# Starting the next group's frequency stage inside the end of the sort, and leaving out the filler matmuls ahead of the first expert tile

## The chip, the cores and the metric

The kernel runs on one core of a Trainium2 chip. The metric is the device time of one execution in microseconds (us); three runs of the kernel before have a median of 2162.24 us (2158.75 to 2167.45). The core has five engines that run their own instruction queues in order: PE (matrix products, with PEld for its weight loads), DVE (vector work), ACT (copies, activations), POOL (elementwise work and the indirect scatters) and SP (issues nearly all plain DMAs). They meet only through semaphores.

## The reference, cut to what matters

```python
# x: (8, 5696, 128)  h: (5696, 128)      L = 2 * 5696
Xf = np.fft.rfft(x, n=L, axis=1); Hf = np.fft.rfft(h, n=L, axis=0)
y = np.fft.irfft(Xf * Hf[None], n=L, axis=1)[:, :S]        # causal convolution
tok = y.reshape(8 * 5696, 128)
e = argmax(tok @ w_gate)                                   # one expert of 8 per token
p = softmax(tok @ w_gate)[e]
out[token] = p * (relu(tok @ w1[e]) @ w2[e])               # w1 128x1024, w2 1024x128
```

## The kernel before, in words

The eight batches are cut into three groups of 2, 3 and 3 (g = 0, 1, 2). The convolution of a group runs in three stages. `phase_a` (for g = 1 and 2 as a `Guest`) multiplies by the 119-point matrix and stores U to DRAM. `phase_b` is the 48-point stage: 120 frequencies, for g = 1 and 2 one per step; four frequencies share one set of loads (`load_m`: the matrix `mt`; `load`: the data `uq` of 576 KB, the inverse matrix `mi` twice 72 KB, the filter `hh` twice 192 KB). A step n issues the forward matmul of frequency n (`forward`, tile `xp`), the DVE product of frequency n - 1 (three operations, the first writes `zt`), the sum of n - 2, the inverse matmul of n - 4 (`vp`) and the copy of n - 5, and then yields to the planner. `phase_c` is the second 119-point stage, which here is called the sort: it makes the tokens, computes logits, ranks every token within its expert, and scatters the rows with POOL into the sorted array SR.

The expert layers (`pipeline`) work on tiles of 256 sorted rows, four steps to a tile (k = 0 to 3). A step does six `mh` matmuls (first layer), the ACT and DVE halves of the relu (`hs`), and six `ma` matmuls (second layer) of two steps earlier. The four quarters of an expert's weights are loaded by `load_w` (`wb`, 512 KB each); from the second tile on, each of these loads is conditional and moves nothing when the tile has the same expert as the one before. `load_w` reads two registers from a table on SP first. There is one set of weight buffers in the parts concerned here, so a load can be issued only when the tile before has passed the quarter that it overwrites.

The order of the instructions on every engine is fixed when the program is built. `run` (L1346) holds the streams `rest` (phases B and C), the weight preparation and `experts`, each with a clock of its own; it always advances the one whose clock is lowest and adds to its clock the cost that it yields (an expert step costs STEP = 1420). What a stream issues before the next yield is one block in program order. Inside `phase_c` a sub-step issues its matmuls, yields, and then does the copies and the ranking of that sub-step. The sort of g = 0 has sub-steps at = 0 to 31 with fresh data and ends with 32, 33, 34, 36 and 38; that of g = 1 has 0 to 47 and ends with 48, 49, 50, 52 and 54. `finished` is the sub-step at which the guest (phase A of the next group) was done: 31 for g = 0, 46 for g = 1. Beginning the next group's `phase_b` (`after`) takes place at L943: two calls of `next(after)`, each of which issues one set of loads. In g = 0 these are in sub-steps 36 and 38, in g = 1 in 50 and 52. Its steps begin after the sort, in the loop at L974.

`spin` (L227) issues matmuls on constants into a PSUM bank that nobody reads: 22 at the start of the first `phase_b`, 40 ahead of the transposition of the first expert tile (L1308), 24 ahead of its first layer (L1301).

Names used below for the expert tiles at the end of the second sort, in order: V, W, X, Y. X has the expert of W; Y has another one, so its weights are really loaded.

Of the kernel before, what the change touches and what calls it, by code (L numbers as in the profile page):

```python
# [59 lines left out]
HOLD = 3  # L60
FETCHED = (0, 1)
GUESTED = (0,)
EAGER = (2, 0)
SETTLED = (2840, 8000, 8000)
LEAD = (0, 4, 6)
A3 = (True, True, True)
# [4 lines left out]
LOGIT = (2, 2, 2)  # L71
RARE = 3
XR = 7
SPIN = (22, 40, 24)


@with_exitstack
def conv_moe(ctx: ExitStack, tc: tile.TileContext, I, out, B, S, D, E, F, split):
# [148 lines left out]
    def spin(count):  # L227
        bank = ps.tile([P, 512], F32, tag="cx", name=f"spin{spun[0]}", bufs=4)
        spun[0] += 1
        for k in range(count):  # L230
            nc.tensor.matmul(
                bank, fcr[:, 0, 0], fcr.rearrange("p a c q -> p (a c q)"), start=True, stop=True
            )
# [220 lines left out]
    def phase_b(gr, guest=None):  # L454
        g, cb, cw, nch, QB, QW = gr.g, gr.cb, gr.cw, gr.nch, gr.qb, gr.qw
# [136 lines left out]
            if g:  # L592
                yield STEP * HEAD[g] / 2
        if g == 0:
            spin(SPIN[0])
        for qb in range(2 if g == 0 else 0):
            for k in range(QB):
                filt(qb, k)
# [92 lines left out]
    def phase_c(gr, guest=None, after=None):  # L691
        g, nb, cb, cw, NI, ns = gr.g, gr.nb, gr.scb, gr.scw, gr.ni, gr.ns
# [9 lines left out]
        nu = NB // NI  # L702

        def load(n):
            if n >= nu:
                return
            vq = sb.tile([PR, 2, NI, gr.cols], F32, tag="ld", name=f"vq{g}_{n}", bufs=LD)
            if g:
                nc.sync.dma_start(vq.rearrange("q c i x -> q (c i) x"), gr.V[:, 2 * n * NI : 2 * (n + 1) * NI, :])
            else:  # L710
                nc.sync.dma_start(vq, gr.V.rearrange("q (c i) x -> q c i x", c=2)[:, :, n * NI : (n + 1) * NI, :])
            vqs[n] = vq.rearrange("q c i x -> q c (i x)")
# [186 lines left out]
        finished, ahead = [None], [0]  # L899
# [4 lines left out]
        for n in range(n_end + 1):  # L904
            for k in range(nsub):
                at = n * nsub + k
                if parts[0].ready and state["prepped"]:
                    state["alone"] = False
                if k == 0:
                    load(n + 2)  # L910
                made = turning = read = carried = None
                if n < nu:
                    made = synth(n, k)
                if TL <= at < total_sub + LL:
                    tp = bank(f"tp{g}_{n}_{k}", "mh")
                if 0 <= at - TL < total_sub:
                    turning = turn(*divmod(at - TL, nsub), tp)
                whole = 0 <= at - LL < total_sub and (at - LL) % nsub == nsub - 1
                if whole:
                    for j in range(nsub):  # L920
                        spare = tp if j else ybank.get((n, k))
                        if spare is None:
                            spare = bank(f"lp{g}_{n}_{k}", "mh")
                        read = logit((at - LL) // nsub, j, spare)
                if k == 0 and n >= sl:
                    score(n - sl, n - sl - 1)
                if guest:
                    few = n < QUIET[g] or k == 0 and n >= sl and not state["alone"] and g
                    carried = guest.begin(1 if few else 2)
                ties = [made, read, carried] if carried and read else [made, turning, read or carried]  # L930
                ties = [x for x in ties if x is not None]
                count = 3 if len(sorts) > 8 else PER_SUB[g]
                for x in ties if len(ties) <= count else ties[:1] + ties[len(ties) - count + 1 :]:
                    sort_one(x)
                if state["alone"]:
                    yield cost if n < nu else cost / 2
                else:
                    yield STEP * (BESIDE if n < nu else ENDING)[g]
                if guest:
                    guest.end()  # L940
                    if guest.m >= guest.M and not guest.over and guest.done():
                        finished[0] = at
                if finished[0] is not None and at >= finished[0] + 4 and n >= nu - EAGER[g] and ahead[0] < 2:  # L943
                    next(after)
                    ahead[0] += 1
                if n < nu:
                    divide(*divmod(at + AHEAD, nsub))
                    settle(n, k)
                if 0 <= at - TL < total_sub:
                    turned(*divmod(at - TL, nsub))  # L950
                for j in range(nsub if whole else 0):
                    logit_out((at - LL) // nsub, j)
                if k == 0:
                    chains = []
                    if 0 <= n - sl - 1 < nu:
                        chains.append(rank(n - sl - 1))
                    if 0 <= n - sl < nu:
                        chains.append(route(n - sl))
                    zipped(*chains)
                    if n - sl - 1 in closes:  # L960
                        pt = closes[n - sl - 1]
                        chores.append(tables(pt, state["base"]))
                        if pt is parts[-1]:
                            chores.append(fill(pt, state["base"]))
                chore(3 if state["alone"] is False else 10)
                if at >= total_sub + LL:
                    break
# [296 lines left out]
    def pipeline(lo, hi):  # L1264
        LAG = 2
        step, nrow, nw, turned = (lo, 0), lo, (lo, 0), lo
        seen, hist, passed = {}, [None] * (LAG + 1), {}
        while True:
            t, k = step
            while nw[0] < min(t + 3, hi) and known(nw[0]):  # L1270
                was, n = user[nw[0]], nw[1]
                if home(nw[0]) and not state["spare"]:
                    break
                if was is not None and was >= lo and passed.get((was, n // 2), -1) < 2 * (n % 2) + 1:
                    break
                load_w(nw[0], n)
                nw = (nw[0], n + 1) if n < 3 else (nw[0] + 1, 0)
            while nrow < min(t + 4, hi) and usable(nrow):
                load(nrow)
                seen[nrow] = len(hist)  # L1280
                nrow += 1
            act = step if t in xts and nw > (t, k // 2) else None
            hist.append(act)
            old, done = hist[-1 - LAG], hist[-2 - LAG]
            to = done[0] if done and done[1] == NPAIR - 1 else None
            ti = turned if turned < nrow and seen[turned] + 2 <= len(hist) else None
            if ti is not None and (act and k < LAG or ti > t + 1 or act is None and ti > t):
                ti = None
            if act is None and old is None and to is None and ti is None:
                state["acting"] = False  # L1290
                leave(len(hist))
                recall(len(hist))
                deliver()
                if t >= hi and not (any(hist[-1 - LAG :]) or pending or leaving or staged or coming or returned):
                    return
                busy = pending or leaving or staged or coming or returned or turned < nrow or any(hist[-1 - LAG :])
                yield STEP if busy else None
                continue
            leave(len(hist))
            recall(len(hist))  # L1300
            if act and step == (0, 0):  # L1301
                spin(SPIN[2])
            if act:
                layer1(t, k)
                state["acting"] = True
                passed[t, 0] = k
            if ti == 0:
                spin(SPIN[1])  # L1308
            if to is not None or ti is not None:
                turn(to, ti)  # L1310
            if old:
                layer2(*old)
                passed[old[0], 1] = old[1]
            yield STEP
            done = None
            if act:
                done = relu(t, k)
                step = (t, k + 1) if k < NPAIR - 1 else (t + 1, 0)
                if k == NPAIR - 1:
                    xts.pop(t)  # L1320
            if ti is not None:
                turned_in(ti)
                turned += 1
            if old and old[1] == NPAIR - 1:
                drain(old[0])
            if to is not None:
                emit(to, len(hist))
            deliver(done)
# [140 lines left out]
```

## Time and profile before

| | before |
|---|---|
| median of three runs | 2162.24 us |
| profiled execution: its time / its span | 2152.79 us / 2151.1 us |
| busy PE, DVE, POOL, ACT | 95%, 72%, 59%, 51% |
| granted TensorE clock, mean | 0.992 |
| PE idle in the span | 2151.1 - 2051.9 = 99 us |

Busy shares are of the span. A row of the timeline gives the start, the time until the last of the merged instructions ended, the engine (SPq is SP's DMA issue), the line, the operation and its tiles, the count, and in brackets how long the engine stood idle ahead of it and for what. A granted clock of 1.00 is 2.4 GHz and 0.5 is 1.2 GHz; a value between is a mean of stretches at the two.

### The profile page before, as it was taken

The page shows a single profiled execution, that of the slowest core. Times are in us where ns is not written, and L with a number is a line of the kernel's source. Part 1 is how long each engine was busy: PE and PEld are TensorE (multiplying, and loading weights), DVE is VectorE, ACT ScalarE, POOL GpSimd, SP SyncE. Part 2 cuts the span into 40 slices and gives each one's busy share as a digit, 9 for nine tenths or more (in the row PEclk, how much of TensorE's full clock was granted, in tenths as well). Part 3 has the DMA queues.
Part 4 walks back from the last instruction along what each step waited for, and adds up shares of the span by engine and source line. Part 5 has one row for each costly group of instructions (what it writes and reads, how often), then busy time and mean ns, then how long its engine had stood idle before and what let it go on. Part 6 is the DMA issues. An engine that isn't in the chain of part 4 may idle for free.

```text
span 2151.1 us, 47076 instructions
## 1 busy us (share of the span) xinstructions
PE 2051.9 (95%) x14284; PEld 1758.3 (82%) x14284; DVE 1557.7 (72%) x3731; ACT 1104.0 (51%) x2359; POOL 1262.3 (59%) x1399
## 2 busy tenths in 40 slices
PE   8899888899999999989999999999999999999998
PEld 5788655666667888876777779999989999999998
DVE  4598745599998789879988885777775555555554
ACT  5688644333334666643434445666644454545444
POOL 6366446466665288882565662688876444444443
PEclk9999999999999999999999999999999999999999
DMA  9899998699998788777898986667645543444441
GB/s 349 280 318 319 316 390 309 197 268 277 285 283 252 281 285 275 260 224 214 243 260 247 253 254 225 209 212 215 199 147 178 170 140 112 140 141 144 144 143 35
DMA packets 236901, 494.39 MB, mean 230 GB/s; under 512 B 33553, under 2 KB 146446, under 8 KB 236647
## 3 DMA queue, kind: packets, MB, share of 16 engines
q1 hardware_dynamic: 212279, 443.06, 65.8%
q0 software_dynamic: 24368, 48.29, 7.0%
q8 instruction: 116, 1.90, 0.4%
q14 instruction: 138, 1.13, 0.2%
HBM read 598.31 MB, written 176.80 MB: 360 GB/s over the span
## 4 chain that ended last, share of the span: by engine, by line
PE 30%; issue 14%; POOL 10%; DVE 7%; DMA 6%; ACT 1%; SPq 1%; POOLq 0%; DVEq 0%; ACTq 0%
PE mh L1164 9%; PE ma L1185 8%; POOL out L1240 8%; PE yp L742 3%; PE vp L564 3%; DMA wb<-WD 3%; PE xp L528 3%; DMA SR<-rt,pi 2%; PE pa L315 2%; POOL SR L656 1%; PE mx L183 1%; DVE hs L1172 1%; PE tp L183 1%; POOL c_fcs L650 1%; ACT hs L1170 1%
## 5 line engine op out<-in xcount | busy, mean ns | idle before, releaser
L1172 DVE SCALAR_TENSOR_TENSOR hs<-mh,hs 128x512 fp32r<-128x512 f32 x728 | 501.1, 690 | 368.9 <-ACT hs L1170 363.9
L1164 PE MATMUL mh<-xtb,wb 128*128 128x256 f32 x4368 | 684.9, 292 | 24.9 <-DMA wb<-WD 12.6
L1170 ACT ACTIVATE hs<-mh 128x512 fp32r<-128x512 f32 x728 | 435.6, 599 | 449.0 <-PE mh L1164 438.0
L1164 PEld LDWEIGHTS mh<-xtb,wb 128*128 128x128 f32 x4368 | 581.6, 189 | 92.2 <-issue 29.4
L1185 PE MATMUL ma<-hs,wb 128*128 128x256 f32 x4368 | 651.5, 285 | 4.5 <-DMA wb<-WD 4.4
L1185 PEld LDWEIGHTS ma<-hs,wb 128*128 128x128 f32 x4368 | 564.4, 189 | 6.3 <-DMA wb<-WD 6.2
L656 POOL DMA_INDIRECT SR<-rt,pi x384 | 398.6, 1038 | 207.3 <-issue 61.9
L1240 POOL DMA_INDIRECT out<-xr x250 | 244.4, 977 | 313.1 <-DVE xr L1203 265.2
L555 POOL TENSOR_TENSOR zt<-zt,xs 128x384 f32<-128x384 f32 (+1 forms) x280 | 298.7, 1076 | 116.2 <-DVE xs L547 87.1
L579 ACT COPY vt<-vp 96x384 f32<-96x384 f32 (+1 forms) x300 | 149.1, 497 | 339.2 <-PE vp L564 332.4
L564 PE MATMUL vp<-zt,mi 128*96 128x384 f32 (+1 forms) x720 | 257.5, 453 | 8.0 <-DVE xs L547 5.6
L528 PE MATMUL xp<-uq,mt 96*128 96x384 f32 (+1 forms) x720 | 256.9, 452 | 3.7 <-ACT vt L579 1.7
L540 DVE TENSOR_TENSOR zt<-xp,hh 128x384 f32<-128x384 f32 (+1 forms) x300 | 173.9, 580 | 47.6 <-PE xp L528 32.5
L564 PEld LDWEIGHTS vp<-zt,mi 128*96 128x96 f32 x720 | 112.4, 162 | 100.6 <-issue 51.0
L1240 POOL DMA_INDIRECT out<-xb x114 | 111.3, 976 | 133.1 <-ACT hs L1170 107.4
L547 DVE SCALAR_TENSOR_TENSOR xs<-xp,hh 64x384 f32<-64x384 f32 (+1 forms) x300 | 175.9, 586 | 6.1
L545 DVE TENSOR_TENSOR xs<-xp,hh 64x384 f32<-64x384 f32 (+1 forms) x300 | 173.3, 578 | 6.0
L315 PE MATMUL pa<-xc,fcr 120*128 120x512 f32 x576 | 166.5, 420 | 10.1 <-DVE rk L867 2.8
L528 PEld LDWEIGHTS xp<-uq,mt 96*128 96x128 f32 x720 | 120.8, 190 | 33.3 <-issue 13.4
L315 PEld LDWEIGHTS pa<-xc,fcr 120*128 120x128 f32 x576 | 101.4, 192 | 43.5 <-DVE rk L867 8.0
L650 POOL TENSOR_TENSOR c_fcs<-c_fcs 120x64 f32<-120x64 f32 (+1 forms) x288 | 126.4, 439 | 6.8
L330 DVE COPY ut<-pa 128x512 f32<-128x512 f32 x96 | 65.8, 687 | 84.5 <-PE pa L315 80.7
(137 smaller groups left out, 2330.1 us busy)
## 6 DMA issues: line engine op xcount, KB each, us to landing
wb<-WD SPq DMA_DIRECT2D x728, 512.0 KB
vq<-VU SPq DMA_DIRECT2D x64, 768.0 KB
VU<-ut SPq DMA_DIRECT2D x48, 768.0 KB
uq<-VU SPq DMA_DIRECT2D x60, 576.0 KB
VU<-vt SPq DMA_DIRECT2D x60, 576.0 KB
xt<-x SPq DMA_DIRECT2D x96, 256.0 KB
xr<-SR SPq DMA_DIRECT2D x182, 130.0 KB
hh<-HS SPq DMA_DIRECT2D x120, 192.0 KB
```

The source lines that it names most:

```text
L315: done = nc.tensor.matmul(banks[m], lhs, rhs, start=(k == 0), stop=(k == len(ops) - 1))
L528: nc.tensor.matmul(xj, mt[:, k0 + j, :], uc.rearrange("p (b d) -> p b d", d=D), start=True, stop=True)
L540: nc.vector.tensor_tensor(out=zt, in0=x3, in1=hv[:, 0].broadcast_to([P] + wide), op=ALU.mult)
L547: nc.vector.scalar_tensor_tensor(out=xs[to], in0=x3[at], scalar=-1.0, in1=him, op0=ALU.mult, op1=ALU.mult)
L555: eng.tensor_tensor(out=zt, in0=zt, in1=xs, op=ALU.add)
L564: nc.tensor.matmul(vp[:K2, j * cw : (j + 1) * cw].rearrange("p (b d) -> p b d", d=D), mi[:, k0 + j, :], zt.rearrange("p b (j d) -> p b j d ...
L656: s = nc.gpsimd.indirect_dma_start(out=SR[:, :], out_offset=IndirectOffsetOnAxis(ap=pi[:, b : b + 1], axis=0), in_=rt[:, b, :], in_offset= ...
L1164: nc.tensor.matmul(hp[:, u, :], wb[:, a, f, :], xt[:, b, :], start=(n == 0), stop=(n == 2))
L1170: done = nc.scalar.activation(hs[:, 0], hp, AF.Relu)
L1172: nc.vector.scalar_tensor_tensor(out=hs[:, 1], in0=hp, scalar=0.0, in1=hs[:, 0].bitcast(F32), op0=ALU.max, op1=ALU.subtract)
L1185: nc.tensor.matmul(accs[t], wb[:, a, f, :], hs[:, b, u, :], start=(k == 0 and u == 0 and n == 0), stop=(k == NPAIR - 1 and u == 1 and n == 2),
L1240: sc = nc.gpsimd.indirect_dma_start(out=out[:, :], out_offset=IndirectOffsetOnAxis(ap=xr[:, s, D + 1 : D + 2].bitcast(I32), axis=0), in_=x ...
```

## The change

The steps of the next group's `phase_b` are called inside the last sub-steps of the sort: in the first of them both sets of loads are issued, in each later one a step. The step's own cost is yielded, so the planner's clock of the stream advances by it. `SOON` replaces `EAGER`: the first call comes in sub-step 32 (g = 0) and 48 (g = 1), the steps 0 to 3 in 33, 34, 36, 38 and in 49, 50, 52, 54. The 64 filler matmuls ahead of the first expert tile are left out; the 22 of the first `phase_b` stay.

```diff
-EAGER = (2, 0)
+SOON = (0, 2)
-SPIN = (22, 40, 24)
+SPIN = 22
...
-                if finished[0] is not None and at >= finished[0] + 4 and n >= nu - EAGER[g] and ahead[0] < 2:
-                    next(after)
+                if after is not None and finished[0] is not None and n >= nu and at >= finished[0] + SOON[g]:
+                    if ahead[0] == 0:
+                        next(after)
+                        next(after)
+                    else:
+                        yield next(after)
                     ahead[0] += 1
...
-            if act and step == (0, 0):
-                spin(SPIN[2])
             if act:
                 layer1(t, k)
...
-            if ti == 0:
-                spin(SPIN[1])
             if to is not None or ti is not None:
                 turn(to, ti)
```

## Rows read from the trace of the kernel before

**Rows 1.** The page, part 1: busy time, share of the span, instructions.
```profile
PE 2051.9 (95%) x14284; PEld 1758.3 (82%) x14284; DVE 1557.7 (72%) x3731; ACT 1104.0 (51%) x2359; POOL 1262.3 (59%) x1399
```

**Rows 2.** Windows, first join and the stage behind: busy by engine, clock, DMA share, GB/s.
```profile
420.00:424.00 4.00, 3.56 (x27) 3.12 (x26) 1.07 (x2) 1.20 (x2) 1.00 (x1) 1.00 0.01 4
...
424.00:427.00 3.00, 2.50 (x23) 2.39 (x22) 2.89 (x22) 1.13 (x4) 1.99 (x2) 1.00 0.97 259
...
421.00:437.40 16.40, 14.00 (x96) 11.68 (x95) 12.60 (x46) 5.22 (x11) 8.02 (x8) 1.00 0.82 189
...
437.00:660.00 223.00, 216.06 (x1048) 144.74 (x1047) 213.72 (x392) 79.28 (x175) 143.83 (x143) 1.00 1.02 279
```

**Rows 3.** Timeline of PE, end of the first sort.
```profile
405.35 9.37 PE L231 MATMUL spin<-fcr 120*128 120x512 f32 x40
...
415.41 5.75 PE L231 MATMUL spin<-fcr 120*128 120x512 f32 x24
421.00 0.87 PE L1164 MATMUL mh<-xtb,wb 128*128 128x256 f32 x6
...
430.66 0.88 PE L528 MATMUL xp<-uq,mt 96*128 96x384 f32 x2 [1.46 <-DMA uq<-VU]
...
435.96 1.58 PE L528 MATMUL xp<-uq,mt 96*128 96x384 f32 x4
```

**Rows 4.** Timeline of SP's DMA issues, end of the first sort.
```profile
407.58 4.47 SPq L1115 DMA_DIRECT2D xr<-SR  x4
412.85 1.92 SPq L1135 DMA_DIRECT2D wb<-WD  x4
...
423.08 0.35 SPq L464 DMA_DIRECT2D mt<-mq  x1
423.48 0.43 SPq L472 DMA_DIRECT2D uq<-VU  x1
...
430.55 0.33 SPq L464 DMA_DIRECT2D mt<-mq  x1
```

**Rows 5.** Waits of SP's queue (429 to 432 us; 957 to 962 us): total, times, longest.
```profile
SPq L464 <- DMA uq<-VU: 1.3, 1, 1.3
...
SPq L479 <- DMA wb<-WD: 2.6, 2, 2.0
```

**Rows 6.** Timeline of DVE, first join: the first operation of the fourth product.
```profile
437.73 0.56 DVE L540 TENSOR_TENSOR zt<-xp,hh 128x384 f32<-128x384 f32 x1
```

**Rows 7.** Timeline of PE, end of the second sort.
```profile
945.28 0.94 PE L1164 MATMUL mh<-xtb,wb 128*128 128x256 f32 x6
...
959.10 1.62 PE L1164 MATMUL mh<-xtb,wb 128*128 128x256 f32 x6 [6.40 <-DMA wb<-WD]
...
966.23 0.91 PE L528 MATMUL xp<-uq,mt 96*128 96x384 f32 x2
...
973.63 1.45 PE L528 MATMUL xp<-uq,mt 96*128 96x384 f32 x4
```

**Rows 8.** Timeline of SP's DMA issues, end of the second sort.
```profile
938.97 0.34 SPq L1115 DMA_DIRECT2D xr<-SR  x1
...
941.65 0.08 SPq L1135 DMA_DIRECT2D wb<-WD  x1
...
943.25 0.08 SPq L1135 DMA_DIRECT2D wb<-WD  x1
...
950.80 0.09 SPq L1135 DMA_DIRECT2D wb<-WD  x1
...
952.35 0.37 SPq L1135 DMA_DIRECT2D wb<-WD  x1
```

**Rows 9.** Windows, second join: columns as in rows 2.
```profile
935.00:940.00 5.00, 5.00 (x54) 4.67 (x51) 3.26 (x16) 3.05 (x9) 4.22 (x7) 1.00 0.17 42
...
955.00:960.00 5.00, 0.90 (x4) 0.94 (x5) 1.79 (x10) 0.00 (x0) 4.17 (x8) 0.54 1.03 356
960.00:965.00 5.00, 5.00 (x36) 5.00 (x35) 2.03 (x6) 2.26 (x5) 4.38 (x7) 0.78 1.09 257
```

More of the change, by code (lines that the diff above doesn't have):

```diff
@@ L594, in phase_b @@
         if g == 0:
-            spin(SPIN[0])
+            spin(SPIN)
         for qb in range(2 if g == 0 else 0):
```

## The prediction

> **What bounds the kernel now.** I read the busy shares first: PE is busy for 2051.9 of 2151.1 us [rows 1], so at most 99 us of idle PE can be won in the whole kernel, and anything that PE does for nobody is a candidate too. Then the windows, stage by stage. The two places that the change touches are the ends of the first and second sort; I call them the first join (405 to 437 us) and the second join (939 to 975 us). In the 48-point stage behind the first join PE is busy for 216.1 and DVE for 213.7 of 223 us [rows 2]: both are the bound at once, so what a join gives or takes is carried on into the stage and not absorbed by it. Last, PE's and SP's timelines in the joins, to see which wait ends last in each. At the first join the filler matmuls make PE look busy; the only visible wait is 1.46 us for `uq`. At the second there is one large wait, 6.40 us for the weights of tile Y [rows 7], after which the granted clock is 0.54 and 0.78 in two windows of 5 us [rows 9], a mixture of 1.2 and 2.4 GHz.
>
> The planner comes before any engine. Let A be the stream's clock in the first sub-step with loads, E the cost of a closing sub-step, c that of a step of the 48-point stage. Before, step k is issued at A + 4E + kc. After, the steps 0 to 3 lie at A + E, A + 2E + c, A + 3E + 2c, A + 4E + 3c, because each step's cost is yielded; step 4 then lies at A + 4E + 4c, exactly where it was. (In the first join the loads stood at sub-steps 36 and 38, and the steps behind 38; the count is the same.) So nothing from step 4 on moves against the experts. The change can only win waits ahead of step 4, and the whole effect can be read from when PE gets to step 4: its forward matmul ended about 437.4 us at the first join [rows 3] and about 975 us at the second [rows 7].
>
> **First join: the filler.** 9.37 + 5.75 = 15.1 us of PE go [rows 3]. What hides them is that the first tile is not there: SP issues its rows from 407.58 to 412.05 and its weights from 412.85 to 414.77 [rows 4], and the DMA has run dry only at 420 (4 GB/s in 420 to 424, rows 2). Four quarters in some 6.3 us are 1.6 us each, so the first quarter's bytes are over at about 415.5; with a lag of 3.5 us (below) it lands before 419. The first layer can thus start 2 to 4 us ahead of 421.0, and not 15.
>
> **First join: step 0.** Its forward matmul now stands in PE's queue directly behind the first `mh` group and ahead of the second. PE is in order: until `uq` has landed, the whole expert tile, the ranking matmuls and what DVE does with them stand behind it. The loads are issued directly behind the four weight loads, so from about 415 instead of 423.08, but their bytes queue behind those of the weights, to 420.1. What a load of `uq` takes: issued at 423.48 into an empty DMA; PE waited for it until 430.66 [rows 3], and SP's next `mt` at 430.55 did too [rows 4, 5]. SP keeps no more than eight loads in flight here, since that `mt` is the eighth issue behind `uq`. The 768 KB of `mt` and `uq` at 259 GB/s [rows 2] are 3.0 us from 424.05, so it landed 3.5 us after its last byte by that count. Now: 420.1 + 2.4 to 3.0 + 3.5 = 426. Bounds: 422.5 if there is no lag at all, 428.6 if the full 1.3 MB of the set must pass first (5 us and 3.5 us). I take 425.5, nearest to the measured landing. The Trainium skill (DMA: Bandwidth & Descriptors, "Anatomy of one DMA") gives about 2 us of fixed cost, most of it the receipt of the last write; by that it would be 424.5 and the join 1 us better; the row shows more, and I go by the row.
>
> From there to step 4 PE has the work it had from 421.0 to 437.4, 14.0 us [rows 2], less the first `mh` group (0.87), and about 0.5 us of short waits: 13.6 us. PE has by then stood for some 6 us. A wait of that length at the second join cost 0.46 x 0.9 + 0.22 x 5.0 = 1.5 us of clock [rows 9]. By PE: 425.5 + 13.6 + 1.5 = 440.6 against 437.4, 3.2 us later. By DVE: its 12.6 us of work less 0.7, behind about 1.6 us for two matmul groups, put the fourth product at 439.0 against 437.73 [rows 6], 1.3 us later. As the stage behind is bound by both, I take the middle, **+2 us**. Bounds: -3 (`uq` never waited for, and only the earlier first layer counts) to +6 (428.6 us, by PE). Without the filler there is nothing that covers this wait.
>
> **Second join: what is won.** Before, the loads of the 48-point stage go to SP between 946.96 and 950.44 and keep the DMA busy when Y's first quarter is issued at 952.35 [rows 8]; it lands at 959, 6.7 us later. After, all twelve loads are issued from about 939.9 (behind the `xr` at 938.97), when the DMA moves 42 GB/s [rows 9]. They are out of Y's way. If that were all, Y's weights would be issued about 2 us earlier and land before 954: the 6.40 us of wait and 1.5 us of clock go, -7.9 us.
>
> **Second join: what is newly queued.** The twelve loads are now ahead of two skipped loads on SP, the last quarter of W (941.65) and the first of X (943.25), for which the first layer of X waits. With eight in flight the tenth of the twelve waits until the first `uq` has landed. By the row above that is 7.0 us after its issue: 940.3 + 7.0 = 947.3. Three issues later (0.45 us each) SP is at 948.6, the last of W goes, and after two register reads (1.6 us between 941.65 and 943.25, rows 8) the first of X at 950.2. X's first `mh` began 2.0 us after that issue before [rows 7, 8] with no wait shown, so 2.0 is an upper bound: 951 to 952.2 instead of 945.28. PE meanwhile has step 0 (from 947.3) and a ranking group. X's two further pairs of steps took 7.4 us to 952.7; with the steps 1 and 2 between them (0.65 us each) PE is through at about 960.5. Y's load follows the end of W's second layer, 3.4 us behind X's start: 955.4, and 1.55 us of reads (950.80 to 952.35), 957. Now into a free DMA: 512 KB at 356 GB/s [rows 9] are 1.4 us, with a lag between 0 and 3.5 us 958.4 to 961.9. So Y starts at 960.5 to 962, 1.4 to 2.9 us later than 959.10, but with three steps (1.95 us) done and no clock loss behind it (1.5 us): -2.0 to -0.5. With a `uq` that lands 1 us sooner, as a DMA with so little to do may give, 1 us is added. I take **-2 us**; bounds -7.9 (SP not held) to +5 (SP held until the second `uq`, some 5 us more, less the 2 us taken above for slack).
>
> Nothing else costs: the steps' own instructions, DMAs and conversions are the same in number, POOL's sums of the first two frequencies lie among scatters, and POOL is not the bound (59%, rows 1).
>
> **Sum:** +2 - 2 = 0. The profiled span stays 2151.1 us, its time 2152.8. That execution lies 9.4 us below the median of the runs shown, 2162.24; the prediction is set on the median: **2162 us**. By about 0.5%, 10.8 us, a measurement of this kernel can tell a change from none.
>
> **Rivals.**
> 1. *The loads come in time* (chance 0.22). For it: at the second join the DMA is empty when they are issued. Against: 7 us from an empty DMA at the first. The first join gives up to -3, the second -7.9 at most; with a `uq` that lands 3 us sooner than taken -1 and -5.5. That is 2151 to 2156, say 2155.
> 2. *The new steps dam up the queue* (0.15), on the other side. One mechanism: step 0 blocks PE until `uq`, and SP's limit of eight blocks the weights behind it. It decides from `uq` landing later than 423.8 us at the first join (break-even of +2 there, 1 to 2 us before 425.5) and later than about 949.3 at the second. With 428.6 and the second `uq` to be waited for: +6 and +5, 2173.
> 3. *The clock stays low* (0.05). Both waits at the first join follow each other with little work between, and without the filler PE would run step 0 to 4 at 1.2 GHz: 13.1 us of work double, +13.1 instead of 1.5, 2174. Against it: at the second join the clock was mostly back in the next 5 us window [rows 9]. The Trainium skill (TensorE: Matmul & The Clock Gate, "What's actually happening") has the low clock as the default, which activity releases; by that rule the filler was worth its place, and the trace agrees as far as the fall after the 6.40 us goes.
> 4. *It does nothing* (0.08): both first waits are set by rows and weights in any case, 2162.
>
> **How the numbers follow.** The forecast has 0.50, with its own range 2155 to 2169 (its two terms moved by 3 to 4 us each). Faster by over 0.5% (below 2151.4): 0.11 from rival 1, where `uq` is early at both joins, and 0.05 from the spread of the forecast and of the runs, 0.16. Slower (above 2173): 0.07 from rival 2, 0.03 from 3, 0.03 from the forecast, 0.13. Same: 0.71. For 8 in 10 the range runs from the early half of rival 1 to rival 2: 2152 to 2172.
>
> **What would show it.** Right: no row of L231 after 103 us; the first `mh` 2 to 4 us ahead of 421.0; the first `xp` of the second group behind it after a wait for `uq` that ends at 425 to 426; at the second join a first `xp` at about 947, SP's skipped loads after it, X's first `mh` at 951, no 6.40 us wait. Wrong: a first `xp` without a wait at either join (rival 1), or Y later than 964 (rival 2), or a granted clock near 0.5 for all of 420 to 440 (rival 3). If step 4 does not come at the same place among the expert steps, the planner count is wrong, and with it all of this.

## The result and the profile after

The changed kernel takes 2169.94 us, the median of 8 runs (2163.68 to 2174.14), beside 2157.45 us for the kernel before in 8 runs of the same session. The ratio is 1.0054 [1.0038, 1.0069]: it is slower by about 12 us. A repeat on another chip gave 1.0060 [1.0042, 1.0078]. The forecast was 2162 us, no change, so it was wrong. That 2169.94 us lies inside its range of 2152 to 2172 is luck: the range was laid around the median of three runs, 5 us above the 2157.45 us of these eight, and a loss of 12 us was not forecast. The profiled run took 2168.2 us with a span of 2166.5, 15.4 us over the span of before.

The first part of the page after, to be held against [rows 1]:

```profile
PE 2051.1 (95%) x14220; PEld 1759.7 (81%) x14220; DVE 1554.4 (72%) x3731; ACT 1103.1 (51%) x2359; POOL 1263.7 (58%) x1399
```

The 64 filler matmuls are gone, 15.1 us of PE's time, and yet PE is busy for as long as before. So the work that is left ran longer, which points to a lower clock (its mean is 0.983, after 0.992). Where, the windows show. I measure a join from the three transposes of the last ranking (`tp`, line 183) ahead of the first new step to the end of the fifth forward pair (step 4). First join and second join of the kernel before; the columns are those of [rows 2]:

```profile
404.82:437.54 32.72, 30.32 (x181) 25.00 (x180) 16.06 (x68) 6.92 (x18) 12.45 (x13) 1.00 0.83 233
935.89:975.08 39.19, 30.58 (x232) 27.78 (x231) 28.09 (x108) 12.60 (x29) 33.40 (x52) 0.91 0.75 204
```

The same two of the kernel after:

```profile
403.52:444.47 40.95, 21.82 (x117) 17.81 (x116) 18.63 (x71) 6.90 (x18) 14.54 (x15) 0.67 0.82 226
943.40:986.64 43.24, 33.41 (x232) 30.09 (x231) 28.40 (x101) 12.70 (x29) 33.71 (x52) 0.88 0.76 202
```

The first join is 8.2 us longer and its granted clock fell from 1.00 to 0.67; the second is 4.1 us longer. The stretch between them (498.4 and 498.9 us) and the one from the second join to the last forward matmul are the same within 0.6 us. What follows that matmul is 3.7 us longer; the change touches nothing there, and I have no cause for it. With a start 1.3 us earlier, -1.3 + 8.2 + 0.5 + 4.1 + 0.2 + 3.7 = 15.4 us.

PE's timeline after, first join:

```profile
415.38 1.62 PE L1168 MATMUL mh<-xtb,wb 128*128 128x256 f32 x6 [4.32 <-DMA wb<-WD]
422.69 1.62 PE L528 MATMUL xp<-uq,mt 96*128 96x384 f32 x2 [5.70 <-DMA uq<-VU]
423.54 2.06 PE L1168 MATMUL mh<-xtb,wb 128*128 128x256 f32 x6
...
438.20 1.65 PE L1168 MATMUL mh<-xtb,wb 128*128 128x256 f32 x6 [3.29 <-DVE hs L1176]
...
441.78 2.69 PE L528 MATMUL xp<-uq,mt 96*128 96x384 f32 x4
```

Against [rows 3]: the first layer starts 5.6 us earlier (415.38 for 421.00), and step 0 has its operand 8 us earlier (422.69 for 430.66). Step 4, the end of the last row, is nevertheless done at 444.47 instead of 437.54. The whole loss arises between step 0 and step 4. The second `mh` group, which follows step 0 at once, is what stood dammed up: without step 0 it runs 1.9 us behind the first (experiment e1_no_filler). DVE over the same stretch, the last row answering to [rows 6]:

```profile
426.31 0.69 DVE L1176 SCALAR_TENSOR_TENSOR hs<-mh,hs 128x512 fp32r<-128x512 f32 x1 [7.89 <-ACT hs L1174]
...
435.87 1.44 DVE L869 TENSOR_TENSOR rk<-rk,oh 120x54 f32<-120x54 f32 x1
437.47 1.28 DVE L1176 SCALAR_TENSOR_TENSOR hs<-mh,hs 128x512 fp32r<-128x512 f32 x2
...
443.30 0.56 DVE L540 TENSOR_TENSOR zt<-xp,hh 128x384 f32<-128x384 f32 x1 [2.95 <-PE xp L528]
```

DVE has nothing to do for 7.89 us, because all that it could do hangs on the matmuls behind step 0. Then it works without a break from 426.31 to 440.3, and PE's `mh` at 438.20 waits for it for 3.29 us with step 3's matmul queued behind; that matmul comes late, and DVE waits 2.95 us in its turn. In the kernel before DVE's activation of the second group was at 423.62, so 14.1 us ahead of the fourth product; now these are 426.31 and 443.30, 17.0 us. DVE starts 2.7 us later and takes 2.9 us longer: that is the whole 5.6 us by which the fourth product is later than in [rows 6]. The clock in windows of 5 us:

```profile
410.00:415.00 5.00, 1.06 (x13) 0.57 (x12) 0.42 (x1) 0.37 (x1) 0.99 (x1) 0.50 0.70 206
415.00:420.00 5.00, 1.62 (x6) 1.36 (x6) 0.69 (x1) 0.90 (x3) 0.99 (x1) 0.50 1.05 387
420.00:425.00 5.00, 2.31 (x7) 1.73 (x8) 0.00 (x0) 0.00 (x0) 0.00 (x0) 0.50 1.07 250
425.00:430.00 5.00, 5.00 (x33) 4.64 (x33) 3.64 (x11) 1.46 (x3) 1.99 (x2) 0.78 1.09 247
430.00:435.00 5.00, 4.23 (x32) 3.64 (x30) 4.73 (x25) 1.97 (x5) 3.02 (x3) 1.00 0.23 63
435.00:440.00 5.00, 1.80 (x8) 1.80 (x9) 4.80 (x12) 0.38 (x2) 2.00 (x2) 0.74 0.51 118
440.00:445.00 5.00, 5.00 (x17) 3.47 (x16) 1.99 (x4) 0.92 (x2) 2.01 (x2) 0.57 0.84 188
```

It is 0.50, the 1.2 GHz level, from 410 to 425, while PE mostly waits, recovers when PE has work, and falls once more with the 3.29 us of wait.

The second join after, PE's timeline, to be held against [rows 7]:

```profile
954.08 0.88 PE L528 MATMUL xp<-uq,mt 96*128 96x384 f32 x2 [1.39 <-DMA uq<-VU]
...
958.25 1.62 PE L1168 MATMUL mh<-xtb,wb 128*128 128x256 f32 x6 [3.01 <-DMA wb<-WD]
...
969.41 1.21 PE L1168 MATMUL mh<-xtb,wb 128*128 128x256 f32 x6 [0.99 <-DMA wb<-WD]
...
985.48 0.31 PE L1048 MATMUL tb<-ge,c_small 8*1 8x90 f32 x2 [2.35 <-DVE ge L1042]
```

The single wait of 6.40 us before tile Y has become several, of 1.39, 3.01, 0.99 and 2.35 us (and one of 1.30 at 979.22). The clock falls behind three of them, where [rows 9] show one fall:

```profile
955.00:960.00 5.00, 1.99 (x11) 1.83 (x10) 0.00 (x0) 0.09 (x1) 4.22 (x7) 0.63 1.08 251
960.00:965.00 5.00, 5.00 (x33) 5.00 (x33) 2.57 (x5) 2.23 (x5) 4.36 (x7) 0.69 0.59 167
...
970.00:975.00 5.00, 5.00 (x29) 4.73 (x28) 3.59 (x8) 1.57 (x3) 4.22 (x8) 0.67 0.73 262
...
985.00:990.00 5.00, 4.52 (x19) 3.64 (x20) 4.69 (x19) 1.44 (x3) 0.33 (x1) 0.70 0.53 144
```

### The profile page after: what moved, and what is told of

Same layout as the page of the kernel before. It is cut to its first block, busy times and chain, and to the rows that moved or that the text cites. A ratio compares the mean times of both kernels' runs of the same rounds, so it can differ in the third digit from the quotient of the medians.

```text
span 2166.5 us, 46950 instructions
## 1 busy us (share of the span) xinstructions
PE 2051.1 (95%) x14220; PEld 1759.7 (81%) x14220; DVE 1554.4 (72%) x3731; ACT 1103.1 (51%) x2359; POOL 1263.7 (58%) x1399
## 3 DMA queue, kind: packets, MB, share of 16 engines
q14 instruction: 139, 1.14, 0.2%
## 5 line engine op out<-in xcount | busy, mean ns | idle before, releaser
L1176 DVE SCALAR_TENSOR_TENSOR hs<-mh,hs 128x512 fp32r<-128x512 f32 x728 | 501.5, 691 | 382.7 <-ACT hs L1174 377.9
L1168 PE MATMUL mh<-xtb,wb 128*128 128x256 f32 x4368 | 692.7, 295 | 30.8 <-DMA wb<-WD 16.1
L1168 PEld LDWEIGHTS mh<-xtb,wb 128*128 128x128 f32 x4368 | 587.8, 191 | 97.9 <-issue 38.0
```

The lines of the kernel that those rows point to most:

```text
L1168: nc.tensor.matmul(hp[:, u, :], wb[:, a, f, :], xt[:, b, :], start=(n == 0), stop=(n == 2))
L1176: nc.vector.scalar_tensor_tensor(out=hs[:, 1], in0=hp, scalar=0.0, in1=hs[:, 0].bitcast(F32), op0=ALU.max, op1=ALU.subtract)
```

## Experiments

The change has three parts: the filler goes, the loads of both first steps are issued earlier in one block of twelve, and the steps 0 to 3 lie between the expert tiles. The experiments take them apart, by part and by join. They ran on other chips than the result, on which the kernel before takes 2184 to 2202 us, so each ratio is against the kernel before on its own chip; twelve runs of a variant give an interval of about 0.002 to either side, 4 us. Join lengths come from one profile each. For the first join that is enough: two profiles of the kernel before gave 32.7 and 33.1 us, two of the changed one 40.9 and 41.1, and four kernels without filler that have this join as before lie between 29.2 and 29.4. For the second it is not: nine profiles of kernels that have this join as before lie between 39.2 and 49.7 us (mean 44.1).

**The three parts.** The kernel before without its filler at the joins:

```
-            if act and step == (0, 0):
-                spin(SPIN[2])
...
-            if ti == 0:
-                spin(SPIN[1])
```

> The kernel before with the 64 filler matmuls left out and nothing else changed. Theory S (the loss of the change comes from issuing the steps of the 48-point stage early, so that the experts queue behind step 0 and then behind the products on DVE): the first mh starts near 415 us instead of 421, the first uq is still waited for until about 430, the second join is as before; time within 2 us of before. Theory F (the loss at the first join comes from the missing filler: the clock falls to 1.2 GHz while the first tile is waited for and what follows runs slowly): the stretch from the end of the sort to step 4 gets 5 to 8 us longer, time 5 to 8 us over before.

0.9985 [0.9970, 1.0000], first join 29.3 us, first `mh` 11.9 us after the join's start instead of 16.2. The filler cost 3.4 us of the join; it was not worth its place there. Theory F, 5 to 8 us over, is excluded.

The changed kernel with the filler put back (the reverse of that edit):

> The changed kernel with the 40 and 24 filler matmuls put back where they were. Theory S: still 8 to 12 us over before, since the filler ends before step 0 is waited for, and the clock falls in that wait all the same. Theory F: the first join is back to its 33.9 us and only the 4 us of the second join are left, time 4 us over before.

1.0034 [1.0013, 1.0056], first join 41.8 us and 7.5 us over in all, between the two expectations. The 33.9 us that theory F had for the join did not come: the filler does not cure the loss.

The changed kernel with the early loads and without the early steps:

```
-                if after is not None and finished[0] is not None and n >= nu and at >= finished[0] + SOON[g]:
+                if after is not None and finished[0] is not None and n >= nu and at >= finished[0] + SOON[g] and ahead[0] < 1:
...
-                    else:
-                        yield next(after)
```

> The changed kernel with both sets of loads early (sub-steps 32 and 48) but the steps 0 to 3 behind the sort as before, without filler. Theory S: no expert work queues behind uq, first join at most 2 us over before; at the second join the first mh of tile X still waits about 3 us for its skipped weight load, which is behind the twelve loads on SP, but the 6.4 us wait for Y is gone: 0 to -3 there; time -3 to +3 of before. Theory F: first join 5 to 8 us longer, time 3 to 8 us over before.

1.0021 [1.0004, 1.0038], first join 34.4 us, 5.1 more than without the filler alone. PE and then SP, first join of this kernel:

```profile
444.54 1.01 PE L1166 MATMUL mh<-xtb,wb 128*128 128x256 f32 x6 [4.39 <-DMA wb<-WD]
```

```profile
438.52 3.32 SPq L475 DMA_DIRECT2D mi<-miq  x2
441.94 0.84 SPq L479 DMA_DIRECT2D hh<-HS  x2
444.31 1.36 SPq L1137 DMA_DIRECT2D wb<-WD  x3
```

The block of twelve holds SP, as I had priced it for the second join, and the weights of the next tile leave only at 444.31; PE waits 4.39 us for them. Neither theory had this wait; the total, 4.6 us over, lies above theory S and within theory F.

The same with the filler:

> As the run with the loads alone early, with the filler in place. Theory S: -4 to 0 us of before, and no more than 2 us from the same kernel without filler. Theory F: -4 to 0 us of before, and 5 to 8 us better than the same kernel without filler.

0.9989 [0.9970, 1.0009], first join 31.9 us, 2.5 less than with the same loads and no filler: the granted clock of the join is 1.00 instead of 0.75, and as the first tile starts later, PE waits 1.07 us for the next weights instead of 4.39. Where a wait follows, the filler did earn something. In the totals the two kernels, on one chip, differ by 0.0032, 7 us, as theory F expected; the join's profile shows 2.5 us of it.

**Join by join.** The changed kernel's code for one sort only, the other join as before, no filler in either (the new branch with `g == 1`, then with `g == 0`):

> The changed kernel with the early loads and steps in the second join alone; the first join has the loads and steps of before and no filler. If the whole loss arises at the first join (theory S): 3 us under before, as with the filler left out alone. If the second join bears the 4 us that the two profiles differ by there (theory J): about 1 us over before.

0.9995 [0.9974, 1.0017], second join 47.1 us. The interval holds both expectations.

> The changed kernel with the early loads and steps in the first join alone; the second join as before. Theory S: 8 to 12 us over before, with 41 us from the first closing sub-step of the sort to step 4 instead of 33. Theory J: 5 to 8 us over before.

1.0030 [1.0004, 1.0056], first join 41.0 us, the length that theory S had; the interval of the total, 1 to 12 us over, holds both theories. Against the kernel without filler (0.9985) the early steps and loads cost some 0.0045, 10 us, at the first join and 0.001, 2 us, at the second. Together with the 3 us that the filler's removal gives this is about 9 of the 12 to 13 us measured. Each of the two differences is uncertain by about 0.003, 6 us, so the loss at the first join is told from none and the 2 us at the second are not.

**Clock or queue at the first join.** Filler between step 0's loads and step 0, to hold the clock while PE waits for `uq`, first 20 matmuls and then 32:

```
                     else:
+                        if g == 0 and ahead[0] == 1:
+                            spin(20)
                         yield next(after)
```

> The changed kernel with 20 filler matmuls put between the first layer's first group and step 0, where PE waits for uq anyway. Theory C (most of the loss at the first join is the granted clock, which falls in that wait; the wait itself and the queue on DVE are the smaller part): the filler ends no later than uq lands, what follows runs at 2.4 GHz, and the join gets 3 to 5 us shorter: 6 to 9 us over before. Theory Q (the queue is the price: the expert steps and their relu halves stand behind step 0 and behind the products): less than 1.5 us shorter, 10 to 12 us over before.

1.0026 [1.0005, 1.0048], first join 41.0 us. Its PE timeline:

```profile
426.25 5.58 PE L231 MATMUL spin<-fcr 120*128 120x512 f32 x20
433.98 0.88 PE L528 MATMUL xp<-uq,mt 96*128 96x384 f32 x2 [2.15 <-DMA uq<-VU]
...
448.64 1.65 PE L1170 MATMUL mh<-xtb,wb 128*128 128x256 f32 x6 [3.29 <-DVE hs L1178]
```

The join is no shorter, as theory Q had it; the total, 5.7 us over, is nearer to theory C. The cover ends 2.15 us before the operand comes, and the next `mh` group still runs 1.64 us, as at 1.2 GHz; hence the longer one:

> The changed kernel with 32 instead of 20 filler matmuls ahead of step 0. With 20 the filler ended 2.2 us before uq landed and what followed still ran at 1.2 GHz, so the clock was not told apart from the queue. With 32 it ends when uq has landed. Theory C (the clock): from step 0 to the end of step 4 14 to 16 us instead of 19 to 22, the join 36 to 38 us. Theory Q (the queue on PE and DVE): 18 us or more, the join 39 us or more, the wait of 3.3 us of the third mh group of tile 2 for DVE still there.

1.0017 [1.0001, 1.0034], first join 42.2 us. PE, then the windows:

```profile
433.70 9.57 PE L231 MATMUL spin<-fcr 120*128 120x512 f32 x32
443.11 0.81 PE L528 MATMUL xp<-uq,mt 96*128 96x384 f32 x2
...
457.22 0.99 PE L1170 MATMUL mh<-xtb,wb 128*128 128x256 f32 x6 [3.29 <-DVE hs L1178]
```

```profile
445.00:450.00 5.00, 3.65 (x28) 3.27 (x27) 4.60 (x20) 1.89 (x5) 1.99 (x2) 1.00 0.74 159
450.00:455.00 5.00, 3.81 (x28) 3.33 (x27) 4.60 (x21) 1.59 (x4) 3.80 (x4) 1.00 0.21 54
```

Now the clock is 1.00 from step 0 to 455, and still it takes 19.2 us from step 0 to the end of step 4 (443.11 to 462.29), with the same wait of 3.29 us for DVE. In the kernel before, with the same matmuls in another order, it takes 15.7 us (below). Without cover the changed kernel took 21.8 us in its first profile and 20.3 in its second (i3_after_again), e2_steps_and_filler 20.5 and f2_first_join 18.9; with 20 matmuls of cover it took 19.6. So the covered ones are 1 us shorter on average, less than the scatter of the others. By these profiles the order makes most of the loss, as theory Q had it, and what the clock adds is not told from the scatter; the totals speak otherwise (i3_after_again). In these windows DVE is busy for 4.60 of 5 us and PE is not: the stretch runs at DVE's pace, and it starts late.

**How many early steps.** The first join alone changed, all loads early, the first step not in sub-step 33 but in 34 and then in 36 (`elif at >= finished[0] + 3`, `+ 5`, ahead of `yield next(after)`):

> First join alone changed, no filler, both sets of loads early, but the first early step in sub-step 34 and so behind the second and third mh groups of the first tile: three early steps. Theory Q (the loss is the one step that stands ahead of the second mh group and makes it, its relu half and all of DVE wait for uq; the products behind it then meet the rankings on DVE): 34 to 37 us at the first join instead of 41, 1 to 4 us over before. Theory L (each early step costs about 1.7 us wherever it stands): 39 us, 5 us over before.

1.0007 [0.9987, 1.0028], first join 33.9 us, as theory Q had it. Step 0 waits for `uq` here too:

```profile
442.22 1.39 PE L529 MATMUL xp<-uq,mt 96*128 96x384 f32 x2 [4.73 <-DMA uq<-VU]
```

But two more `mh` groups and a ranking's matmuls have passed PE ahead of it, DVE has worked off the activation and the ranking behind them before `uq` comes, and PE's later wait for DVE is 0.59 us where it was 3.29.

> As the run with three early steps, with the first in sub-step 36: two early steps. Theory Q: 34 to 35 us, no better than the loads alone early (34.4). Theory L: 37 to 38 us.

0.9994 [0.9977, 1.0011], first join 31.4 us. PE there:

```profile
444.84 0.88 PE L529 MATMUL xp<-uq,mt 96*128 96x384 f32 x2 [0.90 <-DMA uq<-VU]
```

From four early steps to three the join falls by 7 us, from three to two by 2.5, to less than either theory had. It is the one step that stands ahead of the second `mh` group that costs most. The totals (1.0030, 1.0007, 0.9994, the first on another chip) go the same way; their intervals overlap.

One load set at sub-step 32 (33 in the expectation is a slip: `mt` follows the first tile's weights at once, as in all kernels with the early block), the other at 36, no early steps:

> First join alone changed, no filler, no early steps; the first set of loads in sub-step 33 and the second in 36 (before: 36 and 38). If what the early loads cost is that the second tile's weights stand behind twelve loads in SP's queue with eight in flight, six loads leave room: 29 to 31 us at the first join and no wait of over 1 us for wb behind the first one, 2 to 4 us under before. If the loads cost by their bytes ahead of the weights, 32 to 34 us.

First join 28.9 us, the block's 5 us are gone: six loads in a row don't hold SP up against the weights, and PE has no further wait for `wb` in the join. The total, expected 2 to 4 us under, was 1.0010 [0.9988, 1.0031], so the join's gain is not seen in it. One more profile of the kernel before, on this chip, gave the second of the lengths quoted above (33.1 us, and 47.0 at the second join):

> The kernel before once more, for its profile on the chip of these runs: 33 us from the first closing sub-step of the first sort to step 4, 39 to 46 us at the second.

**The second join, and better versions.** No filler, and at the second join one set of loads each at sub-steps 48 and 49, steps as before (`at >= finished[0] + (2 if g else 4)` in the kernel before):

> Without filler, first join otherwise as before; in the second join the first set of loads in sub-step 48 and the second in 49 (before: 50 and 52), no early steps. If what undoes the gain at the second join is that twelve loads in one block hold SP until uq has landed: two sets of six, with the weights of W and X between them, leave SP free, Y's wait for its weights shrinks below 3 us, and the second join takes 36 to 41 us where the late loads take 44 on average; 5 to 9 us under before. If the transfers themselves are the reason: 43 to 46 us, 3 us under before.

0.9972 [0.9953, 0.9990], second join 43.1 us. The waits for weights are 0.92 and 1.14 us there, and the total is 6 us under, as the first expectation had them; the length of the join is that of the second. With 3 us of it from the missing filler, and joins that scatter by 10 us, the gain of the spread loads alone is not shown.

The kernel before with 28 and 16 filler matmuls, then with 20 and 10 (`SPIN = (22, 28, 16)`, `(22, 20, 10)`):

> The kernel before with 28 and 16 filler matmuls instead of 40 and 24: they end about when the rows and the weights of the first tile land, so that the tile is not held up and the clock stays at 2.4 GHz. If both matter, 4 to 6 us under before and a first join of 28 to 30 us with a granted clock above 0.95; if only the start of the tile matters, 2 to 3 us under before.

> The kernel before with 20 and 10 filler matmuls instead of 40 and 24, so that they end before the rows and the weights of the first tile land. Theory C: the first tile starts as early as without filler and at the full clock, 4 to 6 us under before, and 1 to 3 us better than without filler. Theory Q: the clock matters little there, 3 us under before, as without filler.

0.9978 [0.9961, 0.9995] and 0.9979 [0.9958, 1.0000]; first joins 28.8 and 32.7 us. The first is what was expected if both the start of the tile and the clock (1.00) matter; but neither total is told from that without any filler, 0.9985. Spread loads and 28 and 16 together:

> The kernel before with 28 and 16 filler matmuls instead of 40 and 24 at the first join, and at the second join the loads of the 48-point stage two sub-steps earlier, one set in each of two sub-steps. Theory M: at the second join twelve loads in a row were the harm and six at a time are none, so the two gains add up, -5 us from the filler and about -3 us from the loads: a ratio of 0.996, and no wait of 6 us for Y's weights. Theory D: the time of the second join is set by when Y's weights come and scatters by some us whatever the loads do; then the ratio is that of the shorter filler alone, 0.998.

0.9989 [0.9974, 1.0004], joins of 29.5 and 40.5 us, both among the shortest. The largest wait for weights at the second join is 1.83 us. The two gains did not add up to theory M's 0.996, which lies outside the interval; 0.998 lies inside.

Spread loads, and two early steps at the second join (`elif g and ... ahead[0] >= 2: yield next(after)`):

> No filler, the first join else as before; at the second join the loads two sub-steps earlier, one set in each of two sub-steps, and each later sub-step takes one step of the 48-point stage, so that two early steps instead of four stand behind the loads. Theory M: with SP never over eight loads, the first layer of X starts within 4 us of its old place behind the start of the join, and the early steps cost nothing: second join 43 us or less, total like that of the spread loads alone, 0.997. Theory Q, that an early step dams PE's queue here too: step 0 waits for its operand with X's first layer behind it, second join 45 us or more, total 0.999 to 1.001.

1.0005 [0.9986, 1.0024], second join 43.9 us. PE there:

```profile
965.13 0.81 PE L528 MATMUL xp<-uq,mt 96*128 96x384 f32 x2
967.01 0.94 PE L1167 MATMUL mh<-xtb,wb 128*128 128x256 f32 x6 [1.07 <-DMA wb<-WD]
...
976.23 1.62 PE L1167 MATMUL mh<-xtb,wb 128*128 128x256 f32 x6 [5.10 <-DMA wb<-WD]
```

The total is what the theory of the dammed queue expected, the length lies between the two expectations; and step 0 does not wait here, the weights do. This run decides nothing.

> The changed kernel as it is, beside the two others on one chip. So far its ratio and those of its variants with more filler are from different chips. If the clock had a share of the loss, this ratio stays at 1.005, 2 to 4 thousandths above the variants whose step 0 was covered by 20 or 32 filler matmuls (1.0026 and 1.0017). If the order of the queue alone makes the loss, the ratio comes out at 1.002 to 1.003 as theirs. The first join should be 41 us long and the second 43 to 45, as in its first profile.

1.0060 [1.0042, 1.0078], joins of 41.1 and 44.4 us. The totals with step 0 covered, 1.0026 and 1.0017, are lower by 7 to 9 us, on other chips, while their first joins are as long or longer. By the condition set beforehand this gives the clock a share in the loss; the 1 us by which the covered stretches are shorter doesn't account for it, and the profiles don't show the rest.

## Why the prediction was wrong

**First join: the filler (right, a little too small).** The first layer was forecast 2 to 4 us ahead of 421.0. It came 5.6 ahead, 1.3 of which is the earlier start of the join, so 4.3; removing the filler alone shortens the join by 3.4 us.

**First join: when `uq` comes (right mechanism, too pessimistic).** "I take 425.5"; it was taken at 422.69, at the lower bound of 422.5, after a wait of 5.70 us where "some 6" stood. An estimate from the DMA's rates in this profile, 2.41 MB from 412 to 419 us and then 271 and 238 GB/s, puts the last byte of the weights at 418.3, where 420.1 was taken, and that of `mt` and `uq` at 420.8, if they are served in this order; `uq` then landed 1.9 us behind it, where 3.5 was taken.

**First join: from step 0 to step 4 (the step that failed).** The prediction has "13.6 us" of PE work and "1.5 us of clock" behind `uq`. Measured are 21.8 us, from this row of windows after:

```profile
422.69:444.47 21.78, 17.81 (x89) 15.02 (x90) 14.63 (x47) 4.72 (x10) 9.01 (x9) 0.74 0.72 167
```

In the kernel before, at clock 1.00, the same work kept PE busy for 13.27 us:

```profile
421.87:437.54 15.67, 13.27 (x90) 10.99 (x88) 12.74 (x46) 5.22 (x11) 8.02 (x8) 1.00 0.87 200
```

So the work term was right, and the clock costs the other 4.5 us of PE's 17.81, not 1.5. And PE is idle for 21.8 - 17.8 = 4.0 us, 3.29 of them the wait for DVE, where I had 0.5 us of short waits in the 13.6. So 440.6 - 2.8 (`uq` early) - 0.3 (work, and the 0.5 us taken out) + 3.0 (clock) + 4.0 (waits) = 444.5; it was 444.47. The clock term is not steady: PE was busy for 14.6, 16.4 and 17.2 us in this stretch in three other kernels with this order (f2_first_join, i3_after_again, e2_steps_and_filler), 1.3 to 4.0 us over 13.27. The wait of 3.29 us is in all of them.

The same by DVE. I had 1.6 us from `uq` to DVE's start and 11.9 us of work to the fourth product. It was 3.6, since step 0 and the second `mh` group ran at 1.2 GHz (1.62 and 2.06 us); 14.0 us without a break, one ranking operation being 1.2 us longer than usual (below), where the prediction put POOL's sums at nothing because POOL is not the bound; and 2.95 us of waiting for step 3. 422.69 + 3.6 + 14.0 + 2.95 = 443.3, where 439.0 was forecast. Why I missed the wait: I ran PE's and DVE's work side by side and took the middle. But in the order of before, DVE had the second group's activation and two rankings behind it (423.62 to 429.44 us) before `uq` came; with step 0 ahead of the second `mh` group none of this can start, and DVE, which has about as much work in the stretch as PE, becomes the chain. Here the wait at the head of PE's in-order queue is not paid once by PE: DVE, which PE feeds, pays it too.

**First join: SP (not priced).** The limit of eight loads in flight was in the prediction, and used only for the second join. Here it held SP too; these are rows after, SP's issues and its wait:

```profile
411.72 1.92 SPq L1139 DMA_DIRECT2D wb<-WD  x4
...
414.26 0.38 SPq L472 DMA_DIRECT2D uq<-VU  x1
...
420.15 2.74 SPq L475 DMA_DIRECT2D mi<-miq  x2
...
425.62 0.11 SPq L1139 DMA_DIRECT2D wb<-WD  x1
```

```profile
SPq L475 <- DMA uq<-VU: 2.1, 1, 2.1
```

The next weights leave at 425.62, behind the twelve. Here step 0 hides this, since PE stands as well; alone it costs 5.1 us (34.4 against 29.3).

**Second join: the places (right), the gain (wrong).** The join starts 7.5 us later here. Moved by that, the forecast has step 0 at 954.8, X's first layer at 958.5 to 959.7 and Y's at 968.0 to 969.5; measured are 954.08, 958.25 and 969.41. SP's held loads were the reason, as forecast:

```profile
SPq L1139 <- DMA uq<-VU: 1.6, 1, 1.6
```

What failed is "with three steps (1.95 us) done and no clock loss behind it": from Y's start to the end of step 4 should have been 16.0 - 1.95 - 1.5 = 12.5 us, and was 17.2. The clock fell behind the shorter waits too, 5 x 0.33 = 1.65 us in 970 to 975 alone, and PE waited 1.30 and 2.35 us more, the latter for DVE, whose work is as much as before. But the join of before in the profile I predicted from, 39.2 us, is the shortest of nine that have it so, mean 44.1; the six profiles with the block of loads and the early steps have 45.0. The 4.1 us between the two profiles are thus mostly that one profile's luck. The -2 is not seen, in the joins or in the total (0.9995 against 0.9985 without filler); neither is fine enough to exclude it.

**The rivals.** The second, "the new steps dam up the queue", named the right mechanism and about the right time (2173), at 0.15. It had its deciding point wrong: `uq` landed before 423.8, and the join lost 8 us all the same, because the price is not only `uq`'s lateness but what DVE cannot do in the meantime. The third, the low clock, is a part: 4.5 us of PE's busy time in this profile, 1.3 to 4.0 in three others; holding the clock shortened the stretch by 1 us, within the scatter. The Trainium skill (TensorE: Matmul & The Clock Gate, "What's actually happening") has the clock at its low level by default and released by activity; the 0.50 from 410 to 425 agrees. The inference I weighed from it, that the filler was worth its place, does not hold in the old order, which is no slower without it (0.9985). The planner's count was right: step 4 stands at its old place.

**What stays open.** Whether the early steps of the second join cost anything by themselves; how much of the loss the clock makes, since the covered versions are 7 to 9 us better in total than their joins say; and why differences of a join do not reach the total in full (28.9 us of join with 1.0010, 41.0 with 1.0030). The prediction took it that what a join loses is carried on into the stage behind. In the two profiles of the result it is; but the stretch between the joins scatters from 498 to 516 us over all profiles, and is shorter in three kernels with the long first join (499.2, 498.7 and 501.5 us in i3_after_again, f3_cover_step0 and h1_cover_more) than in those of the same chips with a short one (502.8 to 506.2), though not in f2_first_join (504.1). Part of a longer join may be made up there; with one profile each this is not shown. No version tried is faster than the kernel before by 0.5%; the best, spread loads without filler, is at 0.9972.

## What to carry to other kernels

Before a matmul is put ahead of others in PE's queue, list what the other engines do with the matmuls behind it: if its operand is late, their whole work starts late, and where one of them has about as much to do as PE, as here, it becomes the chain: here the operand came 8 us earlier and the stage began 7 us later. Move a step early only to a place behind the last matmul that feeds someone idle: here one sub-step later took away 7 of the 8 us by which the join had grown. A limit found on a queue in one stage may hold in every stage where the same block is issued, as the eight loads of SP did at both joins; price it at each, or issue the block in parts.

## What the runs showed of the hardware

- One VectorE operation was 1.44 us long where its median is 0.217. These are its row over the whole kernel after (min/median/max in ns), and POOL's operation at that time:

```profile
L869 DVE TENSOR_TENSOR rk<-rk,oh x64: 203/217/1437, 295.2 to 1605.0; 120x54 f32<-120x54 f32 x64
```

```profile
436.22 1.00 POOL L555 TENSOR_TENSOR zt<-zt,xs 128x384 f32<-128x384 f32 x1
```

  POOL's sum of two SBUF tensors lies inside it. In the kernel before POOL has only scatters beside the ranking there, and the longest of the 64 is 0.394 us. It is no single event: in all six profiles with four early steps at the first join one of the 64 takes 1.41 to 1.55 us with a POOL sum inside it, and in the 14 others the longest is 0.38 to 0.40. The Trainium skill (GPSIMD Engine Reference, "1. Specifications") has the SBUF interface shared with VectorE and contended by VectorE instructions with two SBUF inputs, as this one is. The runs agree with that. An early step brings its POOL sum next to ranking operations, so about 1.2 us of DVE's chain come with this order; no run moves the sum alone.
- With a wait of 3.29 us on PE the granted clock was 0.74 and 0.57 in two windows of 5 us, and the `mh` group behind it ran 1.65 us instead of about 0.95. In f2_first_join the group behind a wait of the same length ran 0.97 us.
- The chips differ: the same kernel before takes 2157 us on one and 2184 to 2202 on five others.
